# A gated sum of a long convolution and a two-layer network on one core: second-layer bias by accumulating transfers, gate by ScalarE in the last stage, and a front planned with other numbers

## The chip, the core and the metric

The kernel runs on one core of a Trainium2 chip. The core has five engines, each with an instruction stream of its own that is worked off strictly in order: TensorE (PE in the profile), VectorE (DVE), ScalarE (ACT), GpSimd (POOL) and SyncE (SP), which here only starts transfers. POOL and ACT start transfers too. The engines wait for each other through semaphores. The metric is device time in microseconds of one execution, median of several runs.

## The reference

For 2048 positions x of 512 channels (`A_u`), with everything in float32:

```python
g = _sigmoid((x * gate_w).sum(-1, keepdims=True))
a = _A_ref(x, A_A_re, A_A_im, A_B_re, A_B_im, A_C_re, A_C_im, A_log_dt, A_Dskip)
b = _B_ref(x, B_w1, B_b1, B_w2, B_b2)
return g * a + (1 - g) * b
```

`_A_ref` is a convolution over all 2048 positions, channel by channel: its taps are a sum of 128 complex exponentials for each channel and position, the convolution itself is done with a Fourier transform, and `u * Dskip` is added. `_B_ref` is `gelu(x @ w1 + b1) @ w2 + b2` with a hidden width of 1792.

## The kernel before

The program has two parts, `front` and `conv`.

**The front** does three jobs side by side. The generator `dense` computes the network, `taps` the taps with the first stage of their transform, and `signal` the first stage of the transform of x. The network is tiled into 16 blocks `b`: eight blocks of 256 positions, taken twice, since half of the weights (7 of 14 column tiles) fits into SBUF at a time. Blocks 0 to 7 use the first half of the weights and blocks 8 to 15 the second. Every block has four steps `j`, and step `i = 4b + j` has two functions. `hidden(i)` is the first layer for two column tiles (one for `j = 3`): every float32 operand is split into a high part `xh`, `wh` and a low part `xlo`, `wl`, so that a product takes three fast matmuls (L946 to L948) into a PSUM tile `ph`. ScalarE applies gelu in place (L963) and casts the high part to `hh` (L966), VectorE subtracts and leaves the low part in `hl` (L976). There are three `ph` tiles in turn, so step `i + 3` writes a tile only after the `hl` of step `i` has read it. `output(i)` adds the second layer for the two halves `s` of the block into the PSUM tiles `acc` (L994 to L996). For blocks 0 to 7 the first matmul of each `acc` (L989) is the product of `ones` and `b2r`, which puts the bias b2 there. At `j = 3` ScalarE copies `acc` to an SBUF tile `io`, multiplied by the gate 1 - g (L1016). For blocks 0 to 7 SP stores `io` to the output in HBM, and for blocks 8 to 14 POOL sends it there with a transfer that adds to what stands there (L1027). Block 15 and one step of block 14 are left over (`late`), and `conv` does their second layer.

The gate needs the dot products of x with `gate_w`: `dots` does two tiles of 128 positions on VectorE (L870), `gates` makes g and 1 - g from them with a tanh on ScalarE and two sums on VectorE. Before, this is done in three batches early in the front, and the bias tiles are made by `bias`: POOL fills two tiles and loads the row twice, VectorE casts them (L908, L909) and makes the low part (L912).

`taps` makes one sixteenth of the taps at a time. A row of y is set by POOL (L676) and ScalarE (L677), VectorE forms magnitudes (L687) and turns them by the phases (L699, L706, L710), and TensorE sums (`pk`, L724). `prepare` sets up a group of 128 channels, with `pr` holding its parameters (L561).

The order of all this is not the order of the code. Each piece is a task with an engine, a duration that is put in as a number, the tasks it depends on, and a due time. `Plan.run` goes through the tasks in a model of the five engines and hands each engine, when it is free, the ready task that is due first. The order that results is the order of the instructions. The due times come from the constants at the top: `T_0`, `T_MLP` and `W_MLP` spread the steps of the network over time, `K_0`, `T_KG` and `W_KG` the taps, `U_0`, `U_GAP` and `W_U` the signal, and the constants `D_...` shift single kinds of task against these.

**The stage after it**, `conv`, has an order written out by hand: 16 turns `s`. In each, TensorE does the second transform stage of signal (`p2u`) and taps (`p2k`, L1157), VectorE multiplies them, and TensorE transforms back (`pa`, L1196). ScalarE copies `p2k` to `k` (L1165) and `pa` to `sa` (L1202), and in even turns makes the matrix `f1` (tile `f`, L1145 and L1146) that the second half of the next `p2k` needs. SP stores `sa` to `t_d`. In turns 7 to 12 SP loads a pair of output tiles back from HBM into `mos` (`dense`, L1230), in the order 7, 6, 0, 1, 2, 3 of `HERE`; pairs 4 and 5 (`THERE`) follow at the end on ACT's queue. After turn 15 come the left-over second-layer products (`rest`) and then the last stage: 16 tiles of `pb` (L1301), which is the convolution's result. To each, g times it is added to the tile in `mos`, by VectorE (L1313), or for the six tiles of `ASIDE` by ScalarE (L1310) and POOL (L1311), and SP stores each pair (L1317).

Of the kernel before, what the change touches and what calls it, by code (L numbers as in the profile page):

```python
# [17 lines left out]
P = 128  # L18
L = 2048
D = 512  # L20
# [13 lines left out]
T_0 = 22.399  # L34
T_MLP = 408.145
K_0 = 32.114
T_KG = 351.806
U_0 = 29
U_GAP = 18
LAG = 14.812  # L40
TABLE = 27.405
D_KA = -32.407
D_KP = -80.929
D_S1 = 7.912
D_EV = -40.921
D_H = -80.673
D_LO = -23.342
PS = (2, 3, 1, 2)
N_ACC, N_H, N_PK, N_PU = PS
D_SP = -0.52  # L50
MEM = (6, 2, 3)
N_LD, N_HL, N_ST = MEM
D_XS = -157.526
D_G = 1.227
N_WARM = 13
T_EARLY, T_LOFT, T_DEN = 353.026, 381.686, 484.328
Y_K, Y_U = 44.535, 26.725
W_MLP = (-0.0644, -0.031, 0.0179)
W_KG = (-0.0372, -0.0319, -0.0262)
W_U = (-0.0347, -0.139, -0.0186)  # L60
D_MAG = -0.783
D_ROT = 0.578
D_CON = 0.705
D_PHA = 0.305
D_PRE = -3.087
D_XL = 34
D_COE = -3.192
D_OUT = -3.305
D_LAST = -1.557
N_REST = 3  # L70
D_KA0 = 0
D_DT = 5
D_PRM = -277.043
D_D0 = -1024.07
D_WAVE0 = -343.734
D_COE0 = -66.219
D_SP1 = -461.8
D_G0 = 2
D_GW = 598.738
D_XS0 = 98.527  # L80
T_PRE = 0
W_CAST = (0, 0, 0, 0, 0, 0, 0, 0, 1, 1, 0, 1, 0, 0)
X_CAST = (0, 0, 1, 0)
D_X0, D_B2, D_B2C, D_DM = -1313.069, -235.635, -950.754, -4.033
B_CAST = 1
# [222 lines left out]
def gated_mix(  # L308
# [41 lines left out]
    def front(pool, psum, keep, attic, loft, den):  # L350
# [61 lines left out]
        b2r = pool.tile([P, D], F32R, name="b2r")  # L412
        ones = pool.tile([P, P], F32R, name="ones")
# [477 lines left out]
        def bias():  # L891

            k, q = take("ld", N_LD), take("ld", N_LD)
            one, b2f, keys = ld[k][:, 0:P], ld[q], [("ld", k), ("ld", q)]

            def fill():
                nc.gpsimd.memset(b2f, 0.0)
                nc.gpsimd.memset(one, 0.0)
                nc.gpsimd.memset(one[0:1], 1.0)
                nc.gpsimd.memset(one[32:33], 1.0)  # L900

            def rows():
                nc.gpsimd.dma_start(b2f[0:1], b2)
                nc.gpsimd.dma_start(b2f[32:33], b2)

            def go():
                copy = nc.vector.tensor_copy if B_CAST % 2 else nc.scalar.copy
                copy(ones, one)  # L908
                copy(b2r, b2f)  # L909

            def low():
                nc.vector.tensor_sub(b2r[32:33], b2f[32:33], b2r[32:33].bitcast(F32))  # L912

            pl.add("GP", 1.2, fill, D_B2 - 1, [], keys)
            pl.add("GP", 1.2, rows, D_B2, [], keys, wire=(0.2, (2.2, 6.0)))
            if B_CAST % 2:
# [483 lines left out]
```

## Time and profile before

| | us |
|---|---|
| three runs | 519.61, 523.03, 523.76 |
| median | 523.03 |
| profiled execution, device time | 517.95 |
| its span, first to last instruction | 515.7 |
| outside the span | 2.25 |
| busy: TensorE, VectorE, ScalarE, POOL | 501.5, 427.5, 349.6, 42.6 |

The profile is of one execution that took 517.95 us, 5.1 us less than the median of the runs. Its span is 515.7 us; the other 2.25 us lie before the first and after the last instruction. A matmul's shown length overlaps that of the next one, so the pace of TensorE is read from the distance of two starts and not from the length. "PEld" is the loading of weights, which overlaps the matmuls. In what follows a line that begins with a time is from the timeline or from the chain of waits, a line with "x" and "|" is a group of equal instructions, and a line that begins with two times joined by a colon is a stretch of the span with the busy time of each engine, the granted TensorE clock and the DMA share in it.

### The profile page before, as it was taken

Reading aid. Unit: us, or ns where it says so; the run is one execution under the profiler, and the core shown is the slowest. Engines: PE = TensorE matmul, PEld = TensorE weight load, DVE = VectorE, ACT = ScalarE, POOL = GpSimd, SP = SyncE. Lnnn points to the kernel's source line nnn. Section 1 sums busy time; section 2 is a strip of 40 time slices with the busy share of each in tenths; the row PEclk is TensorE's granted clock in tenths of the full one; section 3 lists DMA queues with packets and bytes.
Section 4 is the critical chain, followed back from the end, with each engine's and each line's share of the span. In section 5 each row is a group of like instructions: output and inputs, shape, how many; then the busy total and the mean of one; then the engine's idle time right before and its main releaser. Section 6 shows DMA issues by size and latency. Waiting matters only on the chain.

```text
span 515.7 us, 12196 instructions
## 1 busy us (share of the span) xinstructions
PE 501.5 (97%) x4810; PEld 385.1 (75%) x4810; DVE 427.5 (83%) x792; ACT 349.6 (68%) x625; POOL 42.6 (8%) x82
## 2 busy tenths in 40 slices
PE   7899999999999999999999999999999999999995
PEld 6797898899888989898888977888989742222551
DVE  5999999999999996999999699979951188877543
ACT  5698846899685769995776997747733655555311
POOL 3000000000000000001001020101010100020113
PEclk9899999999999999999999999999999999999999
DMA  8965995522395331565753265967486998999978
GB/s 293 338 229 176 319 310 172 184 85 101 109 219 163 104 124 48 177 217 145 142 186 63 84 143 135 194 205 207 132 231 159 267 391 291 372 319 401 345 280 306
DMA packets 80008, 107.87 MB, mean 209 GB/s; under 512 B 39404, under 2 KB 40560, under 8 KB 79408
## 3 DMA queue, kind: packets, MB, share of 16 engines
q1 hardware_dynamic: 73904, 85.10, 50.9%
q0 software_dynamic: 5120, 18.59, 13.5%
q10 hardware_dynamic: 928, 3.41, 1.8%
q8 instruction: 38, 0.62, 0.5%
q14 instruction: 18, 0.15, 0.1%
HBM read 61.46 MB, written 45.62 MB: 208 GB/s over the span
## 4 chain that ended last, share of the span: by engine, by line
PE 79%; ACT 7%; DVE 7%; DMA 4%; issue 1%; SPq 1%; DVEq 0%; ACTq 0%
PE pk L724 10%; PE ph L946 8%; PE acc L994 8%; PE ph L948 8%; PE ph L947 8%; PE acc L996 7%; PE acc L995 7%; PE p2u L1157 6%; PE p2k L1157 5%; PE pa L1196 3%; PE pb L1301 3%; PE ph L436 3%; DMA tk<-tk_d 1%; DMA tu_d<-attic 1%; DMA sk<-in_w_dram 1%
## 5 line engine op out<-in xcount | busy, mean ns | idle before, releaser
L946 PE MATMUL ph<-xh,wh 128*128 128x256 f32 x448 | 128.1, 286 | 3.2 <-DVE hl L976 2.9
L948 PE MATMUL ph<-xh,wl 128*128 128x256 f32 x448 | 127.6, 285 | 1.4 <-DVE wl L826 1.4
L947 PE MATMUL ph<-xlo,wh 128*128 128x256 f32 x448 | 127.0, 284 | 0.0
L946 PEld LDWEIGHTS ph<-xh,wh 128*128 128x128 f32 x448 | 85.5, 191 | 10.7 <-issue 7.0
L948 PEld LDWEIGHTS ph<-xh,wl 128*128 128x128 f32 x448 | 85.6, 191 | 2.3 <-DVE wl L826 2.3
L947 PEld LDWEIGHTS ph<-xlo,wh 128*128 128x128 f32 x448 | 85.5, 191 | 2.0
L994 PE MATMUL acc<-wh,hh 128*128 128x512 f32 x206 | 83.1, 404 | 0.0
L996 PE MATMUL acc<-wh,hl 128*128 128x512 f32 x206 | 81.0, 393 | 0.9 <-DVE hl L976 0.8
L995 PE MATMUL acc<-wl,hh 128*128 128x512 f32 x206 | 81.1, 394 | 0.0
L963 ACT ACTIVATE ph<-ph,b1t 128x256 f32<-128x256 f32 x112 | 50.5, 451 | 39.2 <-PE ph L948 37.4
L724 PE MATMUL pk<-y,den 128*32 128x64 f32 x2048 | 61.4, 290 | 0.0
L724 PEld LDWEIGHTS pk<-y,den 128*32 128x32 f32 x2048 | 57.2, 136 | 3.5 <-issue 1.8
L976 DVE TENSOR_TENSOR hl<-ph,hh 128x512 fp32r<-128x512 f32 (+1 forms) x62 | 38.1, 616 | 19.2 <-ACT hh L966 19.1
L994 PEld LDWEIGHTS acc<-wh,hh 128*128 128x128 f32 x206 | 39.0, 189 | 16.2 <-issue 8.6
L687 DVE TENSOR_TENSOR y<-y,ea 128x64 f32<-128x64 f32 (+4 forms) x80 | 45.2, 564 | 4.1 <-ACT y L677 3.3
L996 PEld LDWEIGHTS acc<-wh,hl 128*128 128x128 f32 x206 | 38.8, 189 | 10.5 <-DVE hl L976 1.8
L995 PEld LDWEIGHTS acc<-wl,hh 128*128 128x128 f32 x206 | 38.8, 189 | 6.5
L966 ACT CAST hh<-ph 128x512 fp32r<-128x512 f32 (+1 forms) x62 | 33.0, 532 | 13.6 <-PE acc L995 12.0
L530 DVE TENSOR_TENSOR loft<-den,zz 128x256 f32<-128x256 f32 (+2 forms) x48 | 37.2, 775 | 0.6
L531 DVE TENSOR_TENSOR loft<-den,zz 128x256 f32<-128x256 f32 (+2 forms) x48 | 37.1, 773 | 0.0
L699 DVE TENSOR_TENSOR y<-y,loft 128x2048 f32<-128x2048 f32 x16 | 36.5, 2283 | 0.0
L1165 ACT COPY k<-p2k 128x512 f32<-128x512 f32 x32 | 18.7, 585 | 25.1 <-issue 13.1
(194 smaller groups left out, 873.8 us busy)
## 6 DMA issues: line engine op xcount, KB each, us to landing
tu_d<-attic SPq DMA_DIRECT2D x64, 128.0 KB, 3.6
tk_d<-sk SPq DMA_DIRECT2D x32, 256.0 KB, 4.9
t_d<-sa SPq DMA_DIRECT2D x32, 256.0 KB, 5.2
tk<-tk_d SPq DMA_DIRECT2D x24, 256.0 KB, 5.1
t<-t_d POOLq DMA_DIRECT2D x9, 512.0 KB, 7.3
attic<-in_xt_dram SPq DMA_DIRECT2D x16, 256.0 KB, 4.3
attic<-in_xs_dram SPq DMA_DIRECT2D x16, 256.0 KB, 4.6
xh_d<-xh SPq DMA_DIRECT2D x8, 512.0 KB, 3.6
```

Of the source, the lines that this page charges most:

```text
L530: vec(2 * m, lambda: vv.tensor_mul(t, a, br), due, [ka, *kb], [kt])
L687: nc.vector.tensor_mul(both(n, 64 - 3 * n, n), both(0, 64 - n, n), an)
L724: nc.tensor.matmul(pks[q][32 * j : 32 * j + 32, :, gg], x[:, r, :, ch], y[:, r, :, ch], start=(r == 0), stop=(r == 1), skip_group_check=True,)
L946: nc.tensor.matmul(p, h, xh[xk][:, d], start=(d == 0), stop=False)
L947: nc.tensor.matmul(p, h, xlo[xk][:, d], start=False, stop=False)
L948: nc.tensor.matmul(p, lo, xh[xk][:, d], start=False, stop=(d == 3))
L963: nc.scalar.activation(phs[q][:, n], phs[q][:, n], AF.Gelu_apprx_tanh, bias=b1t[:, f : f + 1])
L976: nc.vector.tensor_sub(lo, phs[q][:, 0:nf], hi.bitcast(F32))
L994: nc.tensor.matmul(a, h, wh[1][w], start=start, stop=False)
L995: nc.tensor.matmul(a, h, wl[1][w], start=False, stop=False)
L996: nc.tensor.matmul(a, l, wh[1][w], start=False, stop=(j == 3))
L1157: nc.tensor.matmul(out[64 * i : 64 * i + 64], w, x, start=True, stop=True)
```

## The change

- **Bias.** `bias`, its tiles and its matmul L989 go. A broadcast transfer on SP fills a tile `b2b` with b2 in all 128 rows, and for each of the 16 tiles of blocks 0 to 7 POOL sends `b2b` onto the output tile that SP has just stored, with a transfer that adds.
- **Gate.** `io` is a plain copy of `acc` now. The factor 1 - g is applied by the new function `gated`, on ScalarE and in place, to the pairs that `dense` has loaded: for the pairs of `HERE` at the end of turns 10 to 15, for those of `THERE` in the last stage after the pair `m = 3`.
- **Dot products.** They start at step 6 (`N_G`) and follow each other by 1.255 steps, where they started at step 1, and the gate is made in one batch for all.
- **Front.** Nearly all constants of the plan have other values, and so do two tables of which engine does a cast: three of the four casts of the first two x blocks are VectorE's now, where it was one (`X_CAST`).

```diff
-T_0 = 22.399
+T_0 = 27.471
...
-X_CAST = (0, 0, 1, 0)
+X_CAST = (1, 1, 1, 0)
...
             def products(s, a):
                 ss = slice(s * P, (s + 1) * P)
                 start = j == 0
-                if start and b < NSB:
-                    nc.tensor.matmul(a, ones, b2r, start=True, stop=False)
-                    start = False
...
                     act(
-                        560, lambda n=n, q=q, r=r: nc.scalar.mul(io[r], acc[q], gate[:, 1, n : n + 1]),
-                        t + D_EV, [("acc", q), ("gate", b % NSB)], [("io", r)],
+                        512, lambda q=q, r=r: nc.scalar.copy(io[r], acc[q]),
+                        t + D_EV, [("acc", q)], [("io", r)],
                     )
...
+                        move(
+                            540, lambda n=n: nc.gpsimd.dma_start(out[n], b2b, accum_op=ALU.add), t + D_B2A,
+                            ["b2"], [("v", n)], queue="GP", hold=0.8,
+                        )
...
-            bias()
+            move(256, lambda: nc.sync.dma_start(b2b, b2.to_broadcast([P, D])), D_B2, [], ["b2"])
...
             for b in range(NSB):
-                when.setdefault(1 + min(round(D_G * b), 2 * b), []).append(b)
-            batches = {0: (0, 1), 2: (1, 3), 7: (3, 8)}
+                i = round(N_G + D_G * b)
+                when.setdefault(i if i < 26 else i + 8, []).append(b)
...
-                    dots(k, t + (D_G0 if i < 6 else 0.0))
-                    if k in batches:
-                        gates(*batches[k], t)
+                    dots(k, t + D_G0)
+                    if k == NSB - 1:
+                        gates(0, NSB, t)
...
+        def gated(k):
+
+            for i in range(2):
+                z = mos[k][:, i]
+                nc.scalar.mul(z, z, gate[:, 1, 2 * k + i : 2 * k + i + 1])
...
             turn(s)
             if 7 <= s < 13:
                 dense(HERE[s - 7], nc.sync)
+            if s > 9:
+                gated(HERE[s - 10])
...
             if m < 7:
                 nc.sync.dma_start(out[2 * m : 2 * m + 2].rearrange("s p d -> p s d"), mos[m])
+            if m == 3:
+                for k in THERE:
+                    gated(k)
```

What it makes of the order shows at three places. VectorE's first instructions, before: the low parts of x come first, then four instructions of the time step (`loft`, L491 to L494), the first low part of a weight (`wl`), and the rest of the time step.

```order
L826 TENSOR_TENSOR xlo_107<-attic,xh_105 128x512 x2
L491 TENSOR_SCALAR loft<-pr 128x128
L492 TENSOR_SCALAR loft<-loft 128x128
L493 SCALAR_TENSOR_TENSOR loft<-loft,pr 128x128
L494 SCALAR_TENSOR_TENSOR loft<-loft 128x128
L826 TENSOR_TENSOR wl_123<-sk,wh_109 128x512
L499 TENSOR_TENSOR loft<-loft 128x128
```

Now, at the same place:

```order
L493 SCALAR_TENSOR_TENSOR loft<-loft 128x128
L821 CAST xh_105<-attic 128x512 x2
L498 TENSOR_TENSOR loft<-loft 128x128
L499 TENSOR_TENSOR loft<-loft 128x128
L500 TENSOR_SCALAR loft<-loft 128x128
L501 TENSOR_SCALAR loft<-loft 128x128
L502 CAST loft<-loft 128x128
L503 TENSOR_TENSOR pr<-loft 128x128
L825 TENSOR_TENSOR xlo_107<-attic,xh_105 128x512 x2
L825 TENSOR_TENSOR wl_123<-sk,wh_109 128x512
```

The whole time step stands ahead of the low parts of x now, and VectorE casts x itself; on SP the load of `pr` has moved ahead of that of x, and that of `b2b` ahead of the first weight's. From there to the first `hl` VectorE's order had the three bias instructions L908, L909 and L912 between the low parts of the weights. Now the scaling of `pr` stands there (L560) and, further on, four instructions of the second time step on 4 elements each.

ScalarE in `conv`, at the end of turn 11 and in turn 12, before (`sa` is the copy of turn 11, then `f` for the taps of turn 14, and these taps' copies `k`):

```order
L1202 COPY sa_4767<-pa_5308 128x512
L1202 COPY sa_4768<-pa_5311 128x512
L1145 ACTIVATE f_5337<-cc_5169 64x256
L1146 COPY f_5337<-cc_5169 64x256
L1165 COPY k_5343<-p2k_5340 128x512
```

Now:

```order
L1170 COPY sa_4752<-pa_5295 128x512
L1170 COPY sa_4753<-pa_5298 128x512
L1204 ACTIVATE attic<-attic,gate 128x512 x2
L1113 ACTIVATE f_5326<-cc_5154 64x256
L1114 COPY f_5326<-cc_5154 64x256
L1133 COPY k_5332<-p2k_5329 128x512
```

The two multiplications by the gate have come between the copies of turn 11 and the matrix for turn 12. They wait for the load of pair 6 from HBM.

ScalarE's last instructions, from the loads of the inverse transform on (`den`, `t`), before: behind the loads of pairs 4 and 5 (`loft` and `attic` from `out_dram`) stand the six multiplications by g.

```order
L1216 DMA den<-t_d 32x2048 x2
L1216 DMA t_4777<-t_d 32x4096 x3
L1230 DMA loft<-out_dram 128x2x512
L1230 DMA attic<-out_dram 128x2x512
L1310 ACTIVATE sa_4763<-pb_5507,gate 128x512
L1310 ACTIVATE sa_4764<-pb_5517,gate 128x512
L1310 ACTIVATE sa_4765<-pb_5535,gate 128x512
L1310 ACTIVATE sa_4766<-pb_5545,gate 128x512
```

Now:

```order
L1184 DMA t_4762<-t_d 32x4096 x3
L1204 ACTIVATE loft<-loft,gate 128x512 x2
L1198 DMA loft<-out_dram 128x2x512
L1198 DMA attic<-out_dram 128x2x512
L1286 ACTIVATE sa_4748<-pb_5504,gate 128x512
L1286 ACTIVATE sa_4749<-pb_5514,gate 128x512
L1286 ACTIVATE sa_4750<-pb_5532,gate 128x512
L1204 ACTIVATE loft<-loft,gate 128x512 x2
L1204 ACTIVATE attic<-attic,gate 128x512 x2
L1286 ACTIVATE sa_4751<-pb_5546,gate 128x512
```

The multiplications for pair 3 have come ahead of the two loads, and those for pairs 4 and 5 between the third and the fourth multiplication by g.

On POOL the bias transfers stand in pairs, each ahead of the set-up of a row of y (L676 before, L675 now) or of the reload of an x block (L846, L845). On TensorE the instructions are the same but for the 16 matmuls of the bias; the order of the steps of network, taps and signal against each other differs from the first steps on. Behind the last `pk` there are 144 matmuls of the first layer and 36 of the second now, where there were 132 and 30.

More of the change, by code (lines that the diff above doesn't have):

```diff
@@ L411, in front @@
         dm = pool.tile([P, P], F32, name="dm")
-        b2r = pool.tile([P, D], F32R, name="b2r")
-        ones = pool.tile([P, P], F32R, name="ones")
+        b2b = pool.tile([P, D], F32, name="b2b")
         dts = tiles(4, [P, 4], "dts")
@@ L889, in gates @@
             vec(220, sides, t + D_LO, [], keys)
[L891 to L916, printed above, removed]
-                vec(400, go, D_B2C, keys, ["b2"])
-            else:
-                act(640, go, D_B2C, keys, ["b2"], ops=2)
-            vec(512, low, D_B2C, keys, ["b2"])
         def cols(i):
@@ L1005, in output @@
                 q = (2 * b + s) % N_ACC
-                n = 3 * len(fs) + (1 if j == 0 and b < NSB else 0)
                 mm(
-                    0.2295 * n, lambda s=s, q=q: products(s, acc[q]),
+                    0.2295 * 3 * len(fs), lambda s=s, q=q: products(s, acc[q]),
                     t + LAG + D_OUT * (j == 3) + D_LAST * (b == NB - 2) * j,
-                    [hk, lk, "b2", *ws], [("acc", q)], lat=0.45,
+                    [hk, lk, *ws], [("acc", q)], lat=0.45,
                 )
```

80 lines of the change are left out of this document (40 added, 40 removed).

## The prediction

> **What bounds the kernel now.** I read the page first, then the stretches of the span, then who TensorE waits for, then the timeline where it waits.
>
> ```profile
> PE 501.5 (97%) x4810; PEld 385.1 (75%) x4810; DVE 427.5 (83%) x792; ACT 349.6 (68%) x625; POOL 42.6 (8%) x82
> ```
>
> ```profile
> 8.40:20.00 11.60, 9.86 (x72) 8.84 (x72) 11.37 (x25) 11.06 (x20) 0.69 (x2) 1.00 1.04 376
> 20.00:26.00 6.00, 4.48 (x19) 4.08 (x20) 5.30 (x19) 2.10 (x11) 0.00 (x0) 0.72 0.72 272
> 150.00:200.00 50.00, 50.00 (x634) 44.24 (x633) 44.46 (x79) 36.03 (x64) 1.44 (x5) 1.00 0.40 124
> 250.00:350.00 100.00, 98.05 (x1178) 83.99 (x1170) 90.92 (x164) 76.30 (x130) 10.35 (x19) 1.00 0.59 148
> 409.70:482.20 72.50, 72.50 (x375) 22.30 (x375) 57.06 (x94) 40.04 (x76) 6.31 (x12) 1.00 0.98 353
> 495.90:509.90 14.00, 13.92 (x65) 4.47 (x64) 7.55 (x11) 4.12 (x6) 7.36 (x6) 1.00 0.94 360
> ```
>
> ```profile
> PE ph L946 <- DVE hl L976: 2.9, 2, 1.8
> PE ph L948 <- DVE wl L826: 1.4, 4, 0.6
> PE acc L996 <- DVE hl L976: 0.8, 1, 0.8
> PE acc L989 <- ACT io L1016: 0.4, 1, 0.4
> ```
>
> The columns of a stretch are its length, then busy TensorE, weight loading, VectorE, ScalarE, POOL, the granted TensorE clock, the DMA share and GB/s. TensorE is busy in every later stretch, so what it does is what is paid. It waits in the first 60 us and twice after 250 us (the second wait of 2.9 and that of 0.8), and nearly always for VectorE. Those waits, and the 8.4 us until the first weights are there, are all that a better plan of the front can win. From 410 us on TensorE has no wait to speak of, and the DMA engines are nearly full as well.
>
> **The bias matmuls.** A matmul's shown length overlaps the next, so its price is the distance of starts:
>
> ```profile
> L989 PE MATMUL acc<-b2r,ones 128*128 128x512 f32 x16 | 7.1, 442 | 0.4 <-ACT io L1016 0.4
> 72.48 0.40 PE L994 MATMUL acc<-wh,hh 128*128 128x512 f32 x1
> 72.71 0.40 PE L995 MATMUL acc<-wl,hh 128*128 128x512 f32 x1
> 72.95 0.39 PE L996 MATMUL acc<-wh,hl 128*128 128x512 f32 x1
> ```
>
> One of 512 columns costs 0.235 us (72.48 to 72.95 is two), and 16 cost **-3.7 us**. That it comes through at all rests on TensorE being the bound behind them; the third rival denies this. The transfers that replace them cost TensorE nothing. POOL is busy for 42.6 us of 515.7, and what they store is read back only after 450 us. The 30 copies of `acc` get shorter by about 0.1 us each without the gate, on ScalarE, which bounds nothing there: counted at nothing, covered by TensorE's 100% from 60 us on.
>
> **The start.** TensorE's largest wait ends when VectorE has made the first `hl`:
>
> ```profile
> 7.13 0.23 DVE L491 TENSOR_SCALAR loft<-pr 128x128 f32<-128x128 f32 x1 [1.62 <-DMA pr<-in_prm_dram]
> 7.78 0.62 ACT L824 CAST wh<-sk 128x512 fp32r<-128x512 f32 x1 [2.99 <-DMA sk<-in_w_dram]
> 8.43 0.69 DVE L826 TENSOR_TENSOR wl<-sk,wh 128x512 fp32r<-128x512 f32 x1 [0.16 <-ACT wh L824]
> 12.50 0.42 DVE L909 CAST b2r<-attic 128x512 fp32r<-128x512 f32 x1
> 13.55 0.68 DVE L912 TENSOR_TENSOR b2r<-attic,b2r 1x512 fp32r<-1x512 f32 x1
> 15.47 0.75 DVE L822 CAST wh<-y 128x512 fp32r<-128x512 f32 x2
> 17.36 1.88 DVE wl L826 x3
> 20.77 1.20 DVE hl L976 x2
> 21.52 0.36 PE L946 MATMUL ph<-xh,wh 128*128 128x256 f32 x1 [1.77 <-DVE hl L976]
> 22.36 0.41 PE L948 MATMUL ph<-xh,wl 128*128 128x256 f32 x1
> 22.58 0.41 PE L946 MATMUL ph<-xh,wh 128*128 128x256 f32 x1
> ```
>
> From 8.43 to 21.37 VectorE hardly rests, so the wait's end is a sum over its order. The new order has between the first `wl` and the first `hl`, both counted: 14 `wl` at 0.63 (1.88 for three), 8.8; three casts of weights at 0.38, 1.1; the scaling of `pr`, taken as one more instruction of 512 elements, 0.6; four tiny instructions, an estimate of 0.3 from the 0.23 of one of 128; the `hl`, 0.6. That is 11.4 us. The six instructions of the time step that stood inside have moved ahead of it and the three of the bias are gone. It starts when the first weight is there. That was at 7.78, and the row of `b2b` now lies ahead of it: 256 KB, at the 376 GB/s of this stretch 0.7 us. So the first `wl` comes at about 9.1 and the first `hl` ends at about 20.5 instead of 21.37, 0.9 us earlier. TensorE's order has two second-layer matmuls more ahead of that wait (0.5 us). Against it stands that the casts of x now queue on VectorE behind the load of `pr`, which at 7.13 was late. I take **-1.0 us**. The lower end is the wait and the half clock gone altogether, -3.5: 1.77, and 0.28 of the 6 us with clock 0.72 for the rest. The upper is +1.0, if x and weights come 2 us later than I think.
>
> The half clock is visible in the distance of 22.36 and 22.58, 0.22 where the pace is 0.12. The page "TensorE: Matmul & The Clock Gate" of the Trainium skill (Part 1) says that the clock is halved after an idle window of about 3.4 us. This case's trace differs: one wait of 1.77 us with smaller ones ahead of it sufficed. By the page a wait like this one's would cost no half clock, and the start would gain a further 1.7 us; I go by the trace and leave it in.
>
> **The rest of the front.** The other waits of before, at 45, 53, 304 and 343 us, sum to 2.4 us (0.4, 0.1, 1.1 and 0.8). The new plan has its own. Its order gives VectorE less lead: ahead of the 34th of 62 `hl` stand 409 instructions where there were 400, among them a whole further set of five magnitudes:
>
> ```profile
> L687 DVE TENSOR_TENSOR y<-y,ea 128x64 f32<-128x64 f32 (+4 forms) x80 | 45.2, 564 | 4.1 <-ACT y L677 3.3 <-issue 0.4
> ```
>
> Nine instructions at the mean of 0.54 (427.5 over 792) are 4.9 us. VectorE had slack there: 5.5 of the 50 us from 150 to 200. So the lead is about used up, and I expect waits like those of before or a little more: **+0.4 us**, between -2.4 (none) and +9 (below).
>
> At the end of the front the first load of the taps was just in time; there is now more TensorE work behind the last `pk` (6 and 12 matmuls more), so this does not become a wait.
>
> **The turns of conv.** Two multiplications come into ScalarE's order at the end of turns 10 to 15:
>
> ```profile
> 325.59 1.27 ACT io L1016 x2
> 470.18 1.07 ACT L1202 COPY sa<-pa 128x512 f32<-128x512 f32 x2 [0.39 <-PE pa L1196]
> 471.28 0.41 ACT L1145 ACTIVATE f<-cc 64x256 f32<-64x256 f32 x1
> 471.70 0.40 ACT L1146 COPY f<-cc 64x256 f32<-64x256 f32 x1
> 472.68 1.03 PE L1157 MATMUL p2k<-tk,f 128*64 128x512 f32 x4
> 477.54 0.58 ACT L1165 COPY k<-p2k 128x512 f32<-128x512 f32 x1 [1.68 <-issue]
> 458.26 0.54 SPq L1230 DMA_DIRECT2D attic<-out_dram  x1
> DMA to landing us min/median/max: 4.8/8.5/11.9
> ```
>
> A pair with a gate took 1.27 us. In odd turns ScalarE has 1.7 us until the next `p2k` (before 477.54), which hides it. In turn 12 the matrix `f` stands behind it: it ended at 472.10 and TensorE took it at 472.68, so 1.27 us of delay leave **+0.7 us** of wait. Turn 14 makes no matrix. The pair it needs was asked for at 458.26 and landed after at most 11.9 us, 1.1 us ahead of the multiplication. The bounds are 0 and +3, the latter if the loads come 2 to 3 us later.
>
> **The last stage.** Its end hangs on stores as well as on TensorE:
>
> ```profile
> loft<-out_dram ACTq DMA_DIRECT2D x1, 512.0 KB, 8.2
> 494.61 0.79 ACTq L1230 DMA_DIRECT2D loft<-out_dram  x1
> 495.43 0.65 ACTq L1230 DMA_DIRECT2D attic<-out_dram  x1
> 503.86 0.69 ACT L1310 ACTIVATE sa<-pb,gate 128x512 f32<-128x512 f32 x1 [1.03 <-PE pb L1301]
> 504.62 1.28 POOL L1311 TENSOR_TENSOR loft<-loft,sa 128x512 f32<-128x512 f32 x1 [0.44 <-ACT sa L1310]
> ```
>
> ScalarE now waits for pair 4 (494.61 + 8.2 = 502.8) and does four multiplications, about 2.5 us, before that of 503.86. So that one comes at about 505.4, and POOL's sum and the store of pair 4 1.5 us later. POOL then has 1.28 us of work in each 2.6, and catches up by the last pairs. The DMA engines, at 0.94, have other stores to move meanwhile. **+0.4 us**, between 0 and +1.2, the latter if the loads of pairs 4 and 5, issued 1.3 us later behind pair 3's multiplications, land later too.
>
> **Sum:** -3.7 - 1.0 + 0.4 + 0.7 + 0.4 = -3.2 us on the profiled execution's 517.95, so 514.8. That execution lies 5.1 below the median of the runs; I take the same difference off the median: 523.03 - 3.2 = **519.8 us**.
>
> **The rivals.**
>
> *The plan wins the waits too* (chance 0.17): start and later waits go, -3.7 - 3.5 - 2.4 + 1.1 = -8.5, 514.5 us. For it speaks that VectorE no longer has the bias instructions between the weights; against it that it has the casts of x and is as full as before.
>
> *Slower: VectorE's lead is gone and TensorE waits for it* (0.10). Where the old plan let VectorE idle, 5.5 us of 150 to 200 and 9.1 of 250 to 350, it waited for TensorE or ScalarE; if those waits stay while 4.9 us of lead are gone, TensorE waits for the `hl` behind each, up to about 9 us in all: -3.2 + 9 = +5.8, 528.8 us. It decides from 3.2 us of new waits on; against it speaks that a later order of VectorE also means fewer waits of its own.
>
> *The matmuls' time returns as waits* (0.18): VectorE has about as much work as before, so if it sets the front's pace TensorE only waits longer: about -0.5 + 1.1 = +0.6, 523.6 us. For it speaks that each wait of the front is for VectorE; against it 90 us at a stretch without any.
>
> *ScalarE stands on a late load in conv* (0.08): two loads each 2 us late past their margin give +4 with what lies behind, near 523 us. The median of 8.5 us from issue to landing speaks against it, the longest of 11.9 for it.
>
> **How the numbers follow.** A measurement of this kernel tells about 1%, 5.2 us, from no change. My forecast has a chance of 0.47 and an own range of 516.5 to 523. Of it 0.10 lie below 517.8, and of the first rival 0.15, so faster is 0.25. Slower is 0.08 of the second rival and 0.02 each of the last two, 0.12. Within 1% is 0.63. The range leaves out half of the first rival and the second: 514.5 to 526.
>
> **What would show it.** TensorE's second-layer rows without L989, and the front's end, the first `p2k`, at about 405.3 where it was 409.7; the wait for the first `hl` ending near 21 with the clock again near 0.72; a wait of 0.7 us in turn 12 on `f`; the mean turn otherwise unchanged at 4.6 us. I am wrong if the waits for `hl` between 100 and 400 us sum to over 6 us, or if ScalarE waits for loads from the output in conv.

## The result, and the profile after

| | before | changed |
|---|---|---|
| runs at the time of the comparison, us | 518.65, 519.61, 523.03, 523.76 | 511.67, 511.73, 512.11, 512.23 |
| median, us | 521.32 | 511.92 |
| ratio, 95% interval | | 0.985 (0.981 to 0.989) |
| profiled execution: device time / span, us | 517.95 / 515.7 | 512.11 / 509.0 |
| first `p2k`, the front's end | 408.51 | 400.72 |
| from there to the first `pb` (`conv`) | 87.35 | 87.98 |
| from there to the end of the last matmul | 13.95 | 13.95 |
| from there to the span's end | 5.84 | 6.38 |

The changed kernel is 1.5% faster by that ratio. The two medians of the table would give 1.8%, since two of the four runs of before lie above 523; against the 519.8 to 520.2 us of before in the later comparisons it is 1.5 to 1.6%. Of the 6.7 us by which the two profiled spans differ, the front won 7.8, `conv` lost 0.6 and the very end 0.5. The stages begin at these rows of the two timelines, of before first:

```profile
408.51 0.61 PE L1157 MATMUL p2k<-tk,cc 128*64 128x512 f32 x1
...
495.87 0.65 PE L1301 MATMUL pb<-den,g1t 128*64 128x512 f32 x2
```

```profile
400.72 0.65 PE L1125 MATMUL p2k<-tk,cc 128*64 128x512 f32 x2
...
488.70 0.65 PE L1277 MATMUL pb<-den,g1t 128*64 128x512 f32 x2
```

On the page of the changed kernel TensorE is busy 6.4 us less (501.5 before), ScalarE 3.5 more (349.6 before) and POOL, which now sends the bias, 11.8 more (42.6 before); VectorE is busy as before, within 1 us:

```profile
PE 495.1 (97%) x4794; PEld 379.0 (74%) x4794; DVE 426.6 (84%) x787; ACT 353.1 (69%) x635; POOL 54.4 (11%) x92
```

The stretches of the changed kernel, with the columns as before:

```profile
8.40:20.00 11.60, 9.27 (x58) 8.98 (x59) 11.50 (x24) 8.88 (x15) 0.00 (x0) 0.71 1.01 359
20.00:26.00 6.00, 5.76 (x37) 4.87 (x36) 5.11 (x18) 5.91 (x20) 0.00 (x0) 1.00 1.04 392
...
150.00:200.00 50.00, 50.00 (x643) 44.48 (x642) 49.05 (x83) 36.36 (x71) 5.56 (x11) 1.00 0.50 146
...
250.00:350.00 100.00, 100.00 (x1197) 86.38 (x1195) 96.07 (x172) 76.58 (x132) 12.05 (x21) 1.00 0.60 151
```

The half clock has moved ahead of 20 us. VectorE fills 49.05 of the 50 us from 150 on where it filled 44.46, and 96.07 of the 100 from 250 on where it filled 90.92. Whom TensorE waits for in the changed kernel (total, times, longest):

```profile
PE ph L914 <- ACT wh L823: 4.5, 1, 4.5
PE p2k L1125 <- ACT f L1114: 1.3, 2, 0.8
PE pk L1020 <- POOL dm L1015: 1.0, 1, 1.0
PE acc L961 <- DVE hl L944: 0.2, 1, 0.2
PE pk L723 <- DVE y L709: 0.2, 1, 0.2
PE ph L435 <- DVE hl L944: 0.2, 1, 0.2
```

One large wait is left, for the first weight. Of the waits for `hl`, 3.7 us before, 0.4 is left, and none of the later ones of before has come back. To split the front's 7.8 us, take for each matmul the distance to the start of the one before it, less the median distance of the same pair of kinds in both traces; the sum of this is what TensorE lost (the two columns depend on how kinds are told apart, their difference hardly):

| TensorE lost, us | before | changed | difference |
|---|---|---|---|
| until 30 us | 6.4 | 5.5 | -0.9 |
| from 30 us to the front's end | 8.1 | 5.0 | -3.1 |
| 16 matmuls of the bias at 0.23 | 3.7 | | -3.7 |

The question for the experiments is the second row, for which the prediction had +0.4 and at best -2.4. Most of it are single waits: counted in the same way, TensorE lost 0.54 us at 45.26, 0.26 at 53.26, 1.31 at 304.75 and 0.97 at 343.41 in the kernel before, 3.1 in all, and the two largest losses in the changed kernel are 0.45 and 0.40.

### The profile page after: what moved, and what is told of

Same layout as the page of the kernel before. It is cut to its first block, busy times and chain, and to the rows that moved or that the text cites. A ratio compares the mean times of both kernels' runs of the same rounds, so it can differ in the third digit from the quotient of the medians.

```text
span 509.0 us, 12167 instructions
## 1 busy us (share of the span) xinstructions
PE 495.1 (97%) x4794; PEld 379.0 (74%) x4794; DVE 426.6 (84%) x787; ACT 353.1 (69%) x635; POOL 54.4 (11%) x92
## 4 chain that ended last, share of the span: by engine, by line
PE 81%; DVE 10%; ACT 3%; DMA 2%; issue 2%; SPq 0%; DVEq 0%; ACTq 0%
PE pk L723 10%; PE ph L914 9%; PE ph L916 8%; PE ph L915 8%; PE acc L959 8%; PE acc L961 8%; PE acc L960 8%; PE p2u L1125 6%; PE p2k L1125 5%; PE pa L1164 3%; PE pb L1277 3%; PE ph L435 3%; DVE y L686 2%; DVE y L698 2%; DMA sk<-in_w_dram 1%
## 5 line engine op out<-in xcount | busy, mean ns | idle before, releaser
L1133 ACT COPY k<-p2k 128x512 f32<-128x512 f32 x32 | 18.7, 586 | 22.0 <-issue 10.8
```

## The experiments

Each ratio below is to the kernel before, timed between the same runs on the same chip. In these later comparisons the median of before was 519.8 to 520.2 us.

**The bias matmuls alone.** In the kernel before they are left out:

```diff
                 if start and b < NSB:
-                    nc.tensor.matmul(a, ones, b2r, start=True, stop=False)
-                    start = False
+                    pass
```

> The kernel before without the 16 matmuls L989 and nothing else: all orders stay as they were, so the bias b2 is left out of the result. Theory 'priced' (the prediction's own): each matmul costs TensorE 0.23 us and the whole of it comes through, the run is 3.7 us (0.7%) shorter and the front ends at about 404.8 instead of 408.5. Rival 'returns as waits': VectorE sets the pace of the front, so the time is within 1 us of before and the waits of TensorE for hl grow by some 3 us.

Measured: 515.87 us, ratio 0.993 (0.990 to 0.995), so 3.8 us shorter than 519.78. In the changed kernel 16 are put in:

```diff
+                    if start and b < NSB:
+                        nc.tensor.matmul(a, h, wh[1][w], start=True, stop=True)
                     nc.tensor.matmul(a, h, wh[1][w], start=start, stop=False)
```

> The changed kernel with the first matmul of each of the 16 accumulators of blocks 0 to 7 issued twice (the first of the two is overwritten, the result is the same): 16 matmuls of 512 columns are put back on TensorE, the planner isn't told, all orders stay. Theory 'priced': 3.7 us longer than the changed kernel (about 515.6), with TensorE bound everywhere. Rival 'covered': the changed kernel's TensorE has slack where they stand, under 1.5 us longer.

Measured: 515.1 us, ratio 0.991 (0.989 to 0.993), 3.2 us longer than the changed kernel's 511.92; the profiled span is 3.0 longer. The bias matmuls are worth 3 to 4 us in either kernel, and "priced" holds, if not for the whole: without them the profile's first `p2k` started at 405.35, 3.2 us earlier and not 3.7, and TensorE waited 1.1 us longer for `hl` from 26 to 400 us (3.0 in place of 1.9).

**Numbers of the plan, and parts of the change.** First the kernel before with the constants of the changed one, and the reverse:

```diff
-T_0 = 22.399
+T_0 = 27.471
...
-X_CAST = (0, 0, 1, 0)
+X_CAST = (1, 1, 1, 0)
```

> The kernel before with the plan constants and the X_CAST table of the changed one; bias matmuls, gate with the copy of acc and the three early batches of dot products stay. Theory 'numbers': the waits of TensorE after 26 us (3.1 us of before) went because of the new numbers, so this one is 3 to 4 us faster than before (about 517.5). Rival 'structure': they went because the bias instructions and the early gate left the front, and the new numbers alone give nothing or are worse: 520 to 526 us.

```diff
-T_0 = 27.471
+T_0 = 22.399
...
-X_CAST = (1, 1, 1, 0)
+X_CAST = (0, 0, 1, 0)
```

> The changed kernel with the plan constants and the X_CAST table of before (those of dot products and of the two bias transfers stay new). Theory 'numbers': the waits of the front come back, 3 to 4 us slower than the changed kernel (about 515.5). Rival 'structure': within 1 us of the changed kernel (512 us), since the bias instructions and the early gate are what made VectorE late.

Measured: 525.44 us (ratio 1.012, 1.009 to 1.014) and 524.68 us (1.009, 1.006 to 1.013). "Numbers" fails in the first run, where "structure" allowed 520 to 526; in the second run both fail, since "structure" said 512. Numbers without parts and parts without numbers are each slower than before. So the parts were separated. In one kernel the changed one got the bias matmuls and bias instructions back:

```diff
-            move(256, lambda: nc.sync.dma_start(b2b, b2.to_broadcast([P, D])), D_B2, [], ["b2"])
+            bias()
...
+                if start and b < NSB:
+                    nc.tensor.matmul(a, ones, b2r, start=True, stop=False)
+                    start = False
```

> The changed kernel with its plan constants, the late dot products and the gate in conv, but the bias again by 16 matmuls L989 and VectorE's casts, known to the planner. Theory 'bias': the new numbers were fitted to the front without the bias instructions, and this one alone makes the front wait again: 3.7 us for the matmuls and 4 us or more of waits, 519 to 524. Rival 'gate': the bias costs its matmuls and the instructions at the start, 515 to 517, and the misfit of the 525 us that new numbers in the kernel before gave comes from the early dot products and the gate.

In another it got the early dot products and the gate with the copy of `acc`:

```diff
-                        512, lambda q=q, r=r: nc.scalar.copy(io[r], acc[q]),
+                        560, lambda n=n, q=q, r=r: nc.scalar.mul(io[r], acc[q], gate[:, 1, n : n + 1]),
...
+                when.setdefault(1 + min(round(1.227 * b), 2 * b), []).append(b)
+            batches = {0: (0, 1), 2: (1, 3), 7: (3, 8)}
...
-            if s > 9:
-                gated(HERE[s - 10])
```

> The changed kernel with its plan constants and the accumulating bias transfers, but the dot products early in three batches and the gate again with the copy of acc, as before (the bias is then added without its gate). Theory 'bias': the gate's place matters little, 512 to 514. Rival 'gate': early dot products and the gate that each copy waits for are what the new numbers don't fit, 518 to 522.

The same two edits were made on the changed kernel with the constants of before, the second of them for the first of these two:

> The kernel before, with its plan constants, its early dot products and its gate, and of the change only the bias by accumulating transfers (it is then added without its gate). The planner knows, so its order changes. Theory 'fit' (the constants hold for the set of tasks they were found with): the 3.7 us of the matmuls are won and as much or more is lost in new waits, 519 to 525. Rival 'part': the part gains by itself, 514 to 517.

> The kernel before with its plan constants and its bias matmuls, and of the change only the late dot products and the gate in conv. Theory 'fit': waits of the front grow, 522 to 528. Rival 'part': late dot products by themselves relieve VectorE at the start, 517 to 520.

In a last one only the steps of the dot products were put back:

```diff
-                i = round(N_G + D_G * b)
-                when.setdefault(i if i < 26 else i + 8, []).append(b)
+                when.setdefault(1 + min(round(1.227 * b), 2 * b), []).append(b)
...
-                    dots(k, t + D_G0)
+                    dots(k, t + (2 if i < 6 else 0.0))
```

> The changed kernel with nothing but the dot products back at their early steps (the gate stays one batch and in conv; bias and constants new). If the 9 us that the early gate cost came from the early dot products: 518 to 522. If from the copies of acc that wait for the gate: 512 to 514.

Medians in us, and the start of the first `p2k` in the profile:

| plan constants | bias | dots and gate | median | first `p2k` |
|---|---|---|---|---|
| before's | before's | before's | 519.85 | 408.5 |
| before's | new | before's | 525.95 | 417.4 |
| before's | before's | new | 532.94 | 421.9 |
| before's | new | new | 524.68 | 412.4 |
| new | before's | before's | 525.44 | 415.7 |
| new | new | before's | 521.13 | 413.8 |
| new | before's | new | 530.31 | 417.4 |
| new | new | new | 511.92 | 400.7 |

The two kernels in which constants and parts belong together are the two fastest; the six mixtures are slower than both, the one of 521.13 by little (ratio to before 1.003, 1.000 to 1.005). "Fit" holds, though its upper ends of 525 and 528 us were too low by 1 and 5; "part" and "numbers" don't. With the bias matmuls back the changed kernel is slower than both theories allowed (530.31); with the early dot products and gate it lies where "gate" had it (521.13). Early dot products alone cost the changed kernel 6.5 us (518.42, ratio 0.998, 0.995 to 1.000), so of the 9.2 that dots and gate cost together most comes with the place of the dot products. TensorE's work differs by 3.7 us at most over the eight, and the time by 21: the rest comes with the order that the planner makes.

**Does VectorE have a reserve?** For six x blocks the low part is made twice, in both kernels:

```diff
-            return vec(
-                512, lambda: nc.vector.tensor_sub(lo, src, h.bitcast(F32)), due, [key, hk], [lk]
-            )
+            def low():
+                for _ in range(twice + 1):
+                    nc.vector.tensor_sub(lo, src, h.bitcast(F32))
+
+            twice = hk[0] == "xh" and due > 0
+            return vec(512, low, due, [key, hk], [lk])
```

> The changed kernel with the subtraction that makes the low part of x issued twice for x blocks 2 to 7 (the second writes the same): 12 instructions of 0.6 us more on VectorE between 49 and 200 us, 7.2 us in all, orders unchanged. Theory 'lead used up' (the prediction's step for the rest of the front: VectorE's lead is about gone, so what is put on VectorE comes out as waits of TensorE): 4 to 7 us longer, 516 to 519. Rival 'lead left': VectorE waits for others often enough between 49 and 200 us to take it in, under 1.5 us longer.

> The kernel before with the same 12 subtractions for x blocks 2 to 7 issued twice, orders unchanged: 7.2 us more on VectorE between 28 and 200 us (the changed kernel got 6.3 us longer by it). Theory 'holes': before, VectorE had holes in which to take such work in (5.5 us of 150 to 200, 3.7 of them one wait at 199.78), so it gets at most 3.5 us longer, 523. Rival 'no reserve': 6 to 7 us longer as in the changed kernel, 526 to 527.

Measured: the changed kernel gets 6.3 us longer (518.24, ratio 0.997, 0.994 to 1.000), the kernel before 4.7 (524.52, ratio 1.009, 1.006 to 1.012). So 4.7 lies outside both ranges of the second run, "holes" (at most 3.5) and "no reserve" (6 to 7), and "lead used up" holds for the changed kernel. Set matmul by matmul against the same kernel without the added work, TensorE is later by:

| us later, at a matmul that stood at | 150 us | 200 us | 300 us |
|---|---|---|---|
| before (10 of the 12 by 134 us, the last at 175) | 3.7 | 4.6 | 4.6 |
| changed (9 of the 12 by 150 us, the last at 163) | 2.9 | 6.0 | 6.2 |

In the kernel before, the hole that was to take the work in stands behind all of it, and it is hardly smaller (a hole is a stretch in which VectorE only waits). Without the added work first, then with it:

```profile
199.78 0.69 DVE L976 TENSOR_TENSOR hl<-ph,hh 128x512 fp32r<-128x512 f32 x1 [3.68 <-ACT hh L966]
```

```profile
204.32 0.69 DVE L979 TENSOR_TENSOR hl<-ph,hh 128x512 fp32r<-128x512 f32 x1 [3.35 <-ACT hh L969]
```

The hole came 4.5 us later, as TensorE did by then. So it was no reserve for the work ahead of it. The kernel before took in 2.6 of the 7.2 us; from 60 to 150 us VectorE had idled for 2.2 us (39.60 of 40 busy and 48.24 of 50), in smaller pauses. Nor did TensorE wait behind this hole: its next wait is 105 us later.

**What held VectorE up before.** Whom VectorE waits for between 26 and 350 us, before:

```profile
DVE hl L976 <- ACT hh L966: 6.2, 8, 3.7
DVE loft L584 <- ACT loft L572: 4.9, 2, 4.2
DVE y L687 <- ACT y L677: 3.3, 2, 3.0
DVE pk L741 <- PE pk L724: 2.4, 5, 0.7
```

and in the changed kernel:

```profile
DVE pk L740 <- PE pk L723: 2.9, 7, 0.7
DVE hl L944 <- ACT hh L934: 2.2, 6, 0.8
DVE y L686 <- ACT y L676: 1.5, 4, 0.7
DVE xlo L825 <- ACT xh L823: 0.2, 1, 0.2
```

In these lines its waits for ScalarE fell from 14.4 us to 3.9, and the three long ones are gone. One went without any change of ScalarE's order. The seven products (L572 before, L571 now) stand behind the eleven exponentials as they did, but VectorE has other work until they are there and takes them without a wait, where it had waited 4.2 us:

```profile
281.32 1.51 ACT L571 ACTIVATE loft<-pr 128x128 f32<-128x128 f32 x7
282.97 0.62 DVE L583 TENSOR_SCALAR loft<-loft 128x896 f32<-128x896 f32 x1
```

So VectorE did 10.8 us more of its work by 350 us (before, then changed; the third number is VectorE's):

```profile
26.00:350.00 324.00, 321.56 (x3515) 277.21 (x3517) 304.63 (x578) 253.35 (x449) 17.98 (x38) 1.00 0.55 163
```

```profile
26.00:350.00 324.00, 323.55 (x3624) 279.83 (x3623) 315.38 (x596) 253.60 (x451) 33.79 (x57) 1.00 0.67 182
```

Few such waits are not enough, though. In the kernel before with the new constants, which is 5.6 us slower than before, they are few as well:

```profile
DVE pr L561 <- DMA pr<-in_prm_dram: 4.0, 2, 3.8
DVE hl L976 <- ACT hh L966: 3.9, 7, 1.1
DVE y L687 <- ACT y L677: 1.4, 4, 0.5
DVE wl L826 <- ACT wh L824: 1.0, 1, 1.0
DVE loft L584 <- ACT loft L572: 0.6, 1, 0.6
```

For ScalarE that is 6.9 us and none above 1.1, beside one wait of 3.8 for a load. But TensorE waits 8.2 us from 26 to 400, and half of it not for VectorE, but for ScalarE itself:

```profile
PE ph L946 <- ACT attic L454: 4.0, 1, 4.0
```

From 26 to 400 us it waits 2.3 us in the kernel before and 0.4 in the changed one.

Do those holes make TensorE wait? Two of them are followed, 12 and 5 us later, by the two largest waits of the kernel before behind 30 us:

```profile
292.50 0.63 DVE L584 TENSOR_SCALAR loft<-loft 128x896 f32<-128x896 f32 x1 [4.16 <-ACT loft L572]
...
302.67 0.59 ACT L966 CAST hh<-ph 128x512 fp32r<-128x512 f32 x1
304.01 0.69 DVE L976 TENSOR_TENSOR hl<-ph,hh 128x512 fp32r<-128x512 f32 x1
304.75 0.39 PE L946 MATMUL ph<-xh,wh 128*128 128x256 f32 x1 [1.15 <-DVE hl L976]
...
337.91 0.23 DVE L687 TENSOR_TENSOR y<-y,ea 128x64 f32<-128x64 f32 x1 [2.99 <-ACT y L677]
...
343.41 0.50 PE L996 MATMUL acc<-wh,hl 128*128 128x512 f32 x1 [0.80 <-DVE hl L976]
```

Between 292.50 and 304.75 VectorE does not wait at all. In the kernel before, two tasks of ScalarE were moved behind the planner's back:

```diff
-        for t in pl.run():
+        order = pl.run()
+        ...
+        move_to(tag["exps", 3], order.index(tag["scaled", 3]) + 1)
+        ...
+        move_to(row, order.index(evac))
+        for t in order:
             t.fn()
```

> The kernel before with two tasks of ScalarE moved: the seven products L572 of the last channel group stand ahead of its eleven exponentials L579 instead of behind them, and one row copy L677 stands ahead of the copy L454 that waited 2.91 us at 337.10 for stores to end. Nothing is taken away. In the profile of before VectorE waited 4.16 us for L572 (until 292.50) and 2.99 us for L677 (until 337.91), and TensorE waited for hl 12 us later (1.15 at 304.75) and 5 us later (0.80 at 343.41). Theory 'held up by ScalarE': TensorE pays for those two holes of VectorE, so with them mostly closed both waits go, 2 us shorter (before less 0.4%), and the front's end moves from 408.5 to about 406.5. Rival 'place in the order': the waits come from the long instructions of the taps that stand right ahead of these hl on VectorE, so they stay, within 0.5 us of before.

Measured: 519.44 us against 519.97, ratio 0.999 (0.996 to 1.001), so 0.5 us shorter with "2 us shorter" at the edge of the interval. Its profile says more. VectorE at the two places, and then TensorE's waits from 26 to 405 us:

```profile
289.50 0.63 DVE L585 TENSOR_SCALAR loft<-loft 128x896 f32<-128x896 f32 x1 [0.98 <-ACT loft L573]
293.30 0.23 DVE L688 TENSOR_TENSOR y<-y,ea 128x64 f32<-128x64 f32 x1 [3.17 <-ACT y L678]
...
335.38 0.22 DVE L688 TENSOR_TENSOR y<-y,ea 128x64 f32<-128x64 f32 x1
```

```profile
PE ph L947 <- DVE hl L977: 1.5, 1, 1.5
PE acc L990 <- ACT io L1017: 0.4, 1, 0.4
```

The second hole closed (no wait ahead of 335.38), and TensorE's wait of 0.80 at 343.41 went with it. The first only moved: VectorE waits 0.98 for L573 and then 3.17 for the row copy behind the exponentials, 4.15 in all where it was 4.16, and TensorE's wait stayed, at 1.5 us where it was 1.15. The long instructions of the taps stand ahead of both `hl` as before, so "place in the order" fails for the second wait; for the first the edit decided nothing. For that first wait VectorE can't be the whole cause: ScalarE finished the `hh` that this `hl` reads only at 303.26, and VectorE began the `hl` at 304.01, so a VectorE with nothing else to do would have saved 0.75 of the 1.15 us, an estimate from these rows. Nor did the front's end move to 406.5. The gain reached the last matmul of the first layer (407.72 in place of 408.24), but the first `p2k` then waited for the taps' load and started at 409.29:

```profile
409.29 0.61 PE L1173 MATMUL p2k<-tk,cc 128*64 128x512 f32 x1 [1.28 <-DMA tk<-tk_d]
```

So this run's time could not show what the closed hole is worth.

**The start.**

```diff
-        for t in pl.run():
+        order = pl.run()
+        order.remove(tag["b2b"])
+        order.insert(order.index(ws[-1]) + 1, tag["b2b"])
+        for t in order:
             t.fn()
```

> The changed kernel with the transfer that fills b2b moved on SP behind the 14 loads of the first weights; all else stands in the same order. In the changed kernel the first weight landed at 9.92 us, 0.69 behind b2b (9.23), and TensorE began at 10.62. Theory 'load': the 1.5 us between the second x (7.70) and b2b come back, so TensorE begins at about 9.1 and the run is 1.5 us shorter (510.4). Rival 'VectorE': its order holds the low parts of x until 9.58 to 10.87 behind the time step L498 to L503, so TensorE begins earlier and waits for xlo or later for the first hl instead: within 0.7 us of the changed kernel (511.9).

For the second run also the time step was moved, behind the third of the first low parts:

```diff
+        order.remove(tag["behind"][0])
+        lows = [t for t in order if t in tag["low"][:4]]
+        order.insert(order.index(lows[2]) + 1, tag["behind"][0])
```

> As the one with b2b moved, and on VectorE the six instructions L498 to L503 of the time step (1.5 us) stand behind the low parts of x and the first low part of a weight. Theory 'load': nothing more than b2b alone gave. Rival 'VectorE': now the gain comes, 1.5 to 3 us shorter than the changed kernel (509 to 510.4), TensorE begins before 9 us and the half clock that followed its wait of 4.5 us gets shorter or goes.

Measured: 510.37 us (ratio 0.981, 0.978 to 0.983) and 511.92 us (0.986, 0.982 to 0.991). TensorE with `b2b` moved, its waits at the start:

```profile
7.47 0.38 PE L915 MATMUL ph<-xh,wh 128*128 128x256 f32 x1 [0.87 <-ACT wh L824]
8.59 0.39 PE L916 MATMUL ph<-xlo,wh 128*128 128x256 f32 x1 [0.74 <-DVE xlo L826]
9.80 0.58 PE L917 MATMUL ph<-xh,wl 128*128 128x256 f32 x1 [0.82 <-DVE wl L826]
```

TensorE begins 3.1 us earlier (10.62 in the changed kernel), twice what I expected, and then waits for `xlo` and `wl`. By 30 us it has lost 2.0 us less, but in this profile a wait of 0.89 for `hl` at 331 us and smaller ones gave it back: the first `p2k` starts at 400.72 in both. With the time step moved too, it is 3.4 us ahead at 15 us, and then waits for the first `hl`, in this view of whom it waits for:

```profile
PE acc L964 <- DVE hl L947: 1.7, 1, 1.7
```

It keeps 1.9 us of it up to the first `p2k` (398.78), but its four runs, 508.96 to 515.58, show no gain over the changed kernel, where 509 to 510.4 was expected. So in the profiles both theories had a part: the load was late, and VectorE's sum is next; in the times the second is not shown. The one with `b2b` moved was set beside the changed kernel again:

> The changed kernel again, as the yardstick for the next one on the same chip: about 511.9 us, the ratio to before within 0.981 to 0.989.

> The one with b2b behind the first weights again, beside the changed kernel. If the start's gain comes through: 1.5 us shorter than it. If the front gives it back in waits for VectorE, as the profile of one execution showed: within 0.5 us of it.

512.9 us (0.985, 0.982 to 0.988) and 510.4 us (0.982, 0.979 to 0.985). Side by side the one with `b2b` moved is 2.5 us faster, but the intervals overlap. In this second pair of profiles the wait at 331 us did not come, and the first `p2k` started at 399.50 with `b2b` moved and at 400.54 without. It beats before; that it beats the changed kernel is likely and not settled.

**Turn 12.**

```diff
             if s > 9:
-                gated(HERE[s - 10])
+                for k in ((7,), (), (6,), (0,), (1,), (2, 3))[s - 10]:
+                    gated(k)
```

> The changed kernel with the multiplications of pair 6 at the end of turn 12 in place of turn 11, and those of pairs 0, 1 and 2 one turn later each (pairs 2 and 3 together after turn 15). Theory of the prediction: the wait of 0.69 us on f in turn 12 goes and nothing takes its place, the run is 0.7 us shorter (511.2). Rival: the multiplications in another turn make the copies of pa or p2k late, no change.

Measured: 510.78 us, ratio 0.983 (0.979 to 0.987), too wide for 0.7 us. In the profile the wait in turn 12 is gone (one for `f` of 0.8 us is left, at the first `p2k`), and from the first `p2k` to the first `pb` it takes 87.23 us in place of 87.98. The mixtures with the early gate, which has nothing in turn 11, take 87.23 or 87.24 too, and of the eleven profiles with the gate in turn 11 eight take 87.98 or 87.99. The other three take 88.23, 88.67 and 89.09: two of them wait for the taps' load at the first `p2k` as well, and in the one of 88.67 the wait in turn 12 is longer. Both edits together:

> The changed kernel with both edits that gained alone: b2b behind the first weights and the gate of pair 6 in turn 12. If they add: 0.7 us less than b2b alone (510.4), so 509.7; if the front gives the start's gain back in waits for VectorE, as its profile of one execution showed: 511.

511.33 us (0.985, 0.981 to 0.988): no sum of two gains can be seen. In this one a new wait of 0.3 us came in the last stage, which took 14.45 us where all others took 13.95 or 13.96.

## Why the prediction was wrong, step by step

**The bias matmuls**, -3.7 us: right. Leaving them out gave 3.8, putting them in 3.2. The rival by which their time returns as waits falls; 1.1 us of new waits for `hl` is what is left of it.

**The start**, -1.0: the size was right (-0.9), the path to it was not. I had the first weight later by the 0.7 us that 256 KB take at 376 GB/s. `b2b` held it up by 3.1: with it behind, the first weight landed at 6.78 in place of 9.92 (at 6.79 in place of 9.17 in the second pair). In return TensorE waited for the first `hl` for 0.2 us in place of 1.8, and the half clock stayed, as I had it, but behind the wait for the first weight.

**The rest of the front**, +0.4: this is the step that failed; measured -3.1. I counted nine instructions more on VectorE ahead of the 34th `hl`, set their 4.9 us against 5.5 us of slack between 150 and 200 us, and concluded that the lead is about used up and the waits stay or grow. The slack was used up, as I said: VectorE is busy 49.05 of those 50 us, and 7.2 us of added work came out as 6.3. What failed is the conclusion from a full VectorE to waits of TensorE. None of the waits that I summed to 2.4 us came back in the new order, and nothing took their place beyond 0.4. VectorE's order held instructions that waited for ScalarE, three of them for 3.0 to 4.2 us, and a count of the instructions ahead of an `hl` says nothing of these. In the new order VectorE waits 3.9 us for ScalarE where it waited 14.4. That such a hole made TensorE wait is shown for one, 0.8 us at 343.41. For the wait at 304.75 it is argued, and for at most 0.75 of its 1.15 us; behind the hole at 199.78 TensorE did not wait for 105 us; and the new constants in the kernel before have few waits of VectorE for ScalarE and long waits of TensorE. So what showed in place of my +0.4 is that the waits went, by 3.1 us; why the new order has none stays open for most of it.

Nothing of what I had named as a sign of being wrong came: it was set for waits that grow. The front's end I misread as well: before's first `p2k` starts at 408.51, and 409.7 is the start of its third matmul, held up by the taps' load. It came at 400.72, where my terms put it 4.3 us ahead of before. That the taps' load would not become a wait in the changed kernel was right.

**Constants and parts.** I costed the new constants by what they do to a count of instructions. The table of eight speaks against that: the new constants without one part or both are 9 to 18 us slower than with them. Which of the constants does it stays open.

**The turns of `conv`**, +0.7: right in place and size. The wait came in turn 12, for `f`, and moving the pair's gate takes 0.75 us away.

**The last stage**, +0.4: nothing. The store of pair 4 did go out 1.5 us later against the last matmul, as I said, but it moved nothing: with the gate in the last stage and without it (the mixture with early gate) it takes 13.95 us and 6.38 behind the last matmul. The 0.5 us more at the very end are not the gate's, since that mixture has them too; this part varies from 5.8 to 7.4 over the kernels, and what lengthens it is open.

**The base.** I took -3.2 off a median of three runs, 523.03, which lay 3 us above the median of 15 later runs (519.85). The profiled execution, 517.95, was nearer. Of the 7.9 us by which 519.8 lay too high, about 3 are this and 3.5 the rest of the front; the last stage's 0.4 and the longer very end cancel, and about 1 is not assigned. The range began at 514.5, the price of "the plan wins the waits too"; that rival, -8.5 us, was the nearest to what happened (the spans differ by 6.7 us, the medians of later runs by 7.9), and the same base put it too high. What it gave as its reason, the bias instructions gone from VectorE, is not enough by itself: with the new bias alone the kernel before got slower (525.95). The rival "VectorE's lead is gone" named a true state, as the 12 extra instructions show, but drew the wrong end from it.

## What to carry to other kernels

When a planner's numbers change together with the work that it places, cost neither by itself: the eight kernels spread over 21 us with 3.7 us of difference in TensorE's work. A full engine does not tell whether the engine behind it waits. List whom the pacing engine waits for and, one step back, whom that engine waits for, and ask of each late instruction when its inputs were there: that gives an upper bound for what another order can win at this wait. A pause of an engine is not a reserve for work that is put in ahead of it; the pause moves along. Where a wait goes, look at the next thing that can hold the stage up: here a load took the gain back. Take the base from more than three runs when the effect looked for is smaller than their spread.

## What the runs showed of the hardware

A load that fills 128 rows from one row of 2 KB (256 KB written) held up the loads behind it by 3.1 us in one pair of profiles and by 2.4 in another; at the 376 GB/s of that stretch it would be 0.7.

The granted clock fell at the start after short waits. With `b2b` and the time step moved, TensorE waited 1.60 us at 7.57 and 0.23 at 8.30, and the three stretches from 8.4 to 20 us were:

```profile
8.40:12.00 3.60, 3.60 (x18) 3.60 (x19) 3.46 (x10) 3.00 (x5) 0.00 (x0) 0.55 1.04 393
12.00:16.00 4.00, 4.00 (x36) 4.00 (x35) 4.00 (x8) 3.47 (x6) 0.00 (x0) 1.00 1.07 394
16.00:20.00 4.00, 2.81 (x22) 2.37 (x20) 3.90 (x12) 3.92 (x7) 0.00 (x0) 1.00 1.03 403
```

The clock was 0.55 for 3.6 us with TensorE busy throughout, then full, and the wait of 1.73 us at 20.54 left it at 1.00 in the stretch from 20 to 26 us. In the kernel before, a wait of 1.77 us, 1 us later, halved it. In the changed kernel TensorE began at 10.62 behind its wait of 4.46 us, and its starts stood 0.21 us apart until 15.3 and 0.12 from 15.5 on, so there the clock took 4.8 us to come back. The page "TensorE: Matmul & The Clock Gate" of the Trainium skill (Part 1) says that the clock is halved after an idle window of about 3.4 us and comes back after as long a busy one; the way back agrees with the 3.6 us in the first of these profiles and is shorter than the 4.8 of the changed kernel, and the waits that halved it in the other two were shorter than the page's window.
